# Lightning attention followed by a gated MLP on one core: a new instruction order, and DMA transposes for the last four steps

## The chip, the core and the metric

The kernel runs on one core of a Trainium2 chip. The core has five engines that run side by side and meet through semaphores: PE (TensorE, matrix products), DVE (VectorE), ACT (ScalarE), POOL (GpSimd) and SP (SyncE, which here issues DMAs only). The metric is the device time of one execution in microseconds (us), less is better.

## The reference, cut to what matters

Inputs are q, k, v of shape (4 batches, 8 heads, 768 tokens, 64), one decay per head, and four weights. First comes an attention with decay, block by block; then a gated MLP in which one weight mixes the tokens.

```python
for b in range(nb):                       # blocks of 64 tokens
    intra = einsum('bhic,bhjc->bhij', qb, kb) * Dmask
    intra = einsum('bhij,bhjd->bhid', intra, vb)
    inter = einsum('bhid,bhde->bhie', qb * lam_pow, kv_state)
    out[:, :, sl] = intra + inter
    kv_state = lam_block * kv_state + einsum('bhsd,bhse->bhde', kb * rev_pow, vb)
x = attn_out.transpose(0, 2, 1, 3).reshape(B, S, H * D)
h = maximum(x @ w_in, 0); u, v = h[..., :512], h[..., 512:]
v_n = (v - mean(v)) / sqrt(var(v) + 1e-6)
v_s = einsum('ts,bsd->btd', w_spatial, v_n) + b_spatial[None, :, None]
return (u * v_s) @ w_out
```

## The kernel before

The work is cut into 12 steps n of 256 tokens, three for each of the four batches. The decay is put into the operands: v is scaled by a power per token, q by the inverse power, so that the state only adds up.

The order is written out by hand. `ORDER` is a string of tokens; the last letter names the engine (T is PE, D is DVE, A is ACT, P is POOL, S is SP) and the kernel emits the tokens as they stand, so that every engine runs its own tokens strictly in this order. A token that waits holds everything behind it on its engine. Data dependences and the reuse of buffers become semaphore waits.

A step goes as follows. `LK`, `LQ`, `LV` (L184) each load 512 KB of fp32 over SP's queue into one of three buffers per input. `KC`, `QC` (`split`, L263) cast k and q to bf16 in two halves, one instruction each; `VD` (L274) scales v. `TK`, `TQ` (L284) transpose k and q by eight matrix products each with the identity, into PSUM; `EK` copies kT out, `EQ` (L297) copies qT out and multiplies by the power `lq`. kT and qT have two buffers each. `SC` (L313, two halves of 16 products) makes the scores, `MK` (L317) masks them, `KV` (L329) adds to the state, `SS` copies the state out, `AV` (L350 and L359, two parts) makes the attention output, and `EX` copies it out as x transposed. `PV` (L385, four products of 512 columns) makes the v half of the first weight's product, `PU` (L423, eight of 256) the u half; `EV`, `EU` apply the maximum, and `BN`, `RA`, `RD`, `VN` normalize v.

Once for each batch, after its three steps: `PW` (L445, six products of 384 columns, eight tokens for a batch) mixes the tokens, `GB` adds the bias, `GM` (L456) multiplies by u, `PO` (L462, four products of 512 columns, six tokens) applies the last weight, `EO` copies out and `ST` stores 256 KB over SP's queue.

The first weight comes in two halves, `WI.0` (v half) and `WI.1`, the mixing weight in two, `WS.0` and `WS.1`, the last weight as `WO`. They go over POOL's queue and are cast on the way. Before each stands `GT.x.n`: a copy of one element of the loaded k (x = 0), q (x = 1) or v of step n, which makes POOL wait until that load has landed. `WT` (L435) transposes the mixing weight on PE. At the very start stand the constants: `lam`, `pos`, `idn`, `msk`, and `LB` to `LT`, which make the tables of powers.

Of the kernel before, what the change touches and what calls it, by code (L numbers as in the profile page):

```python
# [21 lines left out]
TQ.2.3.T EK.2.6.A EQ.2.3.D AV.1.0.0.T KV.1.0.T SC.2.1.2.T SC.2.0.4.T SS.1.0.A MK.2.1.2.D KV.1.1.T AV.1.1.0.T  # L22
SS.1.1.A EX.1.1.1.A MK.2.0.4.D LK.5.2.S VD.2.2.P PV.0.1.6.T EX.1.0.0.D PV.0.0.1.T EV.0.1.6.A PV.1.1.0.T
BN.0.1.D PV.1.0.6.T EV.0.0.1.D EV.1.1.0.A BN.0.0.D AV.2.0.2.T EV.1.0.6.A PU.1.1.5.T BN.1.1.D RA.0.A BS.S
GT.0.3.P WS.1.P KV.2.0.T BN.1.0.D PU.1.0.6.T KC.3.2.A SS.2.0.D RD.0.D LK.4.2.S PU.0.0.4.T VN.0.1.D QC.3.2.P
EU.1.1.5.A VN.0.0.D AV.2.1.2.T RA.1.A EU.0.0.4.A GT.1.3.P WS.0.P TK.3.5.T RD.1.D VN.1.0.D EX.2.1.3.A TQ.3.1.T
# [20 lines left out]
EX.6.1.1.A ST.0.3.S TQ.8.6.T RD.5.D MK.7.0.2.D PU.6.1.1.T LK.10.2.S PV.6.0.0.T VN.5.1.D EU.6.1.1.A QC.10.2.P
VN.5.0.D PV.6.1.3.T LK.8.2.S EQ.8.6.D EV.6.0.0.A VD.7.2.P MK.7.1.4.D PW.1.0.1.1.T PU.6.0.6.T LV.11.2.S
BN.6.0.D QC.9.2.P LV.10.2.S PW.1.1.0.0.T GB.1.0.1.1.D EU.6.0.6.A EV.6.1.3.D GM.1.0.1.P PW.1.0.0.6.T
GB.1.1.0.0.D BN.6.1.D GM.1.1.0.P PW.1.2.1.5.T GB.1.0.0.6.D RA.6.A PW.1.3.0.4.T RD.6.D GM.1.0.0.P GB.1.2.1.5.D  # L50
# [459 lines left out]
```

## Time and profile before

| | |
|---|---|
| median of 3 runs | 160.79 us (159.54 to 161.46) |
| the profiled execution | 161.64 us, its span 159.9 us |
| mean granted TensorE clock | 0.979 |
| moved by DMA | 28.63 MB, mean 179 GB/s |
| HBM read, written | 24.77 MB, 6.29 MB |

The span runs from the first to the last instruction of the profiled execution; 1.74 us of that execution lie outside it. Busy time is the union of an engine's instructions. A "[idle before <- releaser]" behind an instruction says how long its engine was idle before it and what ended that.

### The profile page before, as it was taken

How to read it: one execution, taken by the hardware profiler on the slowest of the kernel's cores; microseconds unless marked ns; L12 is line 12 of the kernel's file. 1: busy time of each engine (PE TensorE's matmuls, PEld its weight loads, DVE VectorE, ACT ScalarE, POOL GpSimd, SP SyncE). 2: the span in 40 equal slices, each digit the busy share in tenths (PEclk: the TensorE clock that was granted, in tenths of full speed). 3: DMA queues.
4: the chain of work that ended last, by engine and by line, in shares of the span. 5: the costliest groups of instructions: out<-in, count | busy, mean ns of one | idle time of the engine just before them, and what ended most of it. 6: DMA issues, size and time to landing. Idle time of an engine off the chain costs nothing.

```text
span 159.9 us, 4876 instructions
## 1 busy us (share of the span) xinstructions
PE 138.3 (86%) x2073; PEld 91.0 (57%) x2090; DVE 108.2 (68%) x191; ACT 82.4 (52%) x154; POOL 77.7 (49%) x91
## 2 busy tenths in 40 slices
...
GB/s 104 298 290 290 291 226 230 231 315 237 298 243 240 288 269 235 56 236 195 277 331 318 287 165 71 196 135 0 4 0 6 4 0 4 64 148 186 0 197 197
DMA packets 43448, 28.63 MB, mean 179 GB/s; under 512 B 1058, under 2 KB 40226, under 8 KB 43426
## 3 DMA queue, kind: packets, MB, share of 16 engines
...
q0 software_dynamic: 2384, 2.75, 10.0%
...
q10 hardware_dynamic: 2, 0.00, 0.0%
HBM read 24.77 MB, written 6.29 MB: 194 GB/s over the span
## 4 chain that ended last, share of the span: by engine, by line
PE 54%; DMA 15%; DVE 12%; SPq 5%; POOL 5%; issue 4%; ACT 3%; DVEq 0%; ACTq 0%; POOLq 0%
PE ps L462 13%; PE ps L423 11%; PE ps L385 10%; PE ps L445 8%; DMA win_sb<-in_moe_w_in_dram 6%; SPq L184 5%; DMA q_in<-in_q_dram 5%; DMA k_in<-in_k_dram 5%; POOL gT L456 4%; DVE vsb L450 4%; PE ps L284 3%; DVE vn L414 3%; PE ps L313 2%; PE ps L329 2%; PE ps L359 2%
## 5 line engine op out<-in xcount | busy, mean ns | idle before, releaser
L456 POOL TENSOR_TENSOR gT<-vsb,uT 128x384 bf16<-128x384 f32 x28 | 30.1, 1096 | 28.5 <-DVE vsb L450 23.6
L445 PE MATMUL ps<-wt_sb,vn 128*128 128x384 bf16 x192 | 33.7, 326 | 0.2 <-DVE vsb L450 0.2
L317 DVE TENSOR_TENSOR a_sb<-ps,m 128x1024 bf16<-128x1024 f32 x24 | 28.7, 1218 | 6.0 <-PE ps L313 5.0
L276 POOL TENSOR_TENSOR vd<-v_in,lv 128x1024 bf16<-128x1024 f32 x12 | 22.8, 1904 | 16.0 <-DMA q_in<-in_q_dram 6.4
L385 PE MATMUL ps<-win_sb,xT 128*128 128x512 bf16 x85 | 24.9, 412 | 4.1 <-DMA win_sb<-in_moe_w_in_dram 3.3
L445 PEld LDWEIGHTS <-vn 128*128 128x128 bf16 x192 | 18.2, 98 | 11.9 <-issue 0.4
L423 PE MATMUL ps<-xT,win_sb 128*128 128x256 bf16 x192 | 24.2, 273 | 0.3 <-DVE wt_sb L170 0.3
L168 ACT ACTIVATE o_sb<-ps 128x512 f32<-128x512 f32 x21 | 12.6, 599 | 20.6 <-PE ps L462 17.3
L400 DVE BATCH_NORM_STATS2 st<-vh 128x6 f32<-128x512 bf16 x24 | 16.6, 690 | 9.7 <-ACT vh L390 9.5
L462 PE MATMUL ps<-wout_sb,gT 128*128 128x512 bf16 x90 | 21.6, 379 | 0.3
L450 DVE TENSOR_TENSOR vsb<-ps,bsp 128x384 f32<-128x384 f32 x32 | 17.3, 549 | 5.6 <-PE ps L445 5.1
L423 PEld LDWEIGHTS <-win_sb 128*128 128x128 bf16 x192 | 17.8, 98 | 3.6 <-issue 0.6
L390 ACT ACTIVATE vh<-ps 128x512 bf16<-128x512 f32 x18 | 10.8, 601 | 15.4 <-PE ps L385 15.4
L390 ACT ACTIVATE uT<-ps 128x512 bf16<-128x512 f32 x22 | 12.9, 600 | 10.1 <-PE ps L423 10.1
L385 PEld LDWEIGHTS <-xT 128*128 128x128 bf16 x96 | 9.5, 104 | 14.0 <-issue 6.6
L414 DVE TENSOR_SCALAR vn<-vh,mv,rstd 128x512 bf16<-128x512 bf16 x24 | 16.5, 723 | 0.3
L172 POOL CAST qc<-q_in 128x512 bf16<-128x512 f32 x16 | 9.4, 616 | 14.9 <-DMA q_in<-in_q_dram 10.5
L462 PEld LDWEIGHTS <-gT 128*128 128x128 bf16 x96 | 9.1, 98 | 10.2 <-POOL gT L456 0.3
L168 ACT ACTIVATE xT<-ps 128x512 bf16<-128x512 f32 x19 | 10.7, 597 | 6.4 <-PE ps L359 6.3
L172 POOL CAST kc<-k_in 128x512 bf16<-128x512 f32 x14 | 8.2, 614 | 11.7 <-DMA k_in<-in_k_dram 5.3
L297 DVE TENSOR_TENSOR qT<-ps,lq 128x1024 bf16<-128x1024 bf16 x12 | 8.2, 681 | 7.4 <-ACT kT L168 3.3
L284 PE MATMUL ps<-ident,kc 128*128 128x128 bf16 x96 | 8.2, 235 | 4.7 <-ACT kc L168 4.3
...
## 6 DMA issues: line engine op xcount, KB each, us to landing
k_in<-in_k_dram SPq DMA_DIRECT2D x12, 512.0 KB, 7.4
q_in<-in_q_dram SPq DMA_DIRECT2D x12, 512.0 KB, 7.8
v_in<-in_v_dram SPq DMA_DIRECT2D x12, 512.0 KB, 8.6
out_dram<-o_sb SPq DMA_DIRECT2D x24, 256.0 KB, 2.1
wsp_raw<-in_moe_w_spatial_dram POOLq DMA_DIRECT2D x2, 576.0 KB, 10.0
win_sb<-in_moe_w_in_dram POOLq DMA_DIRECT2D x2, 512.0 KB, 10.2
wout_sb<-in_moe_w_out_dram POOLq DMA_DIRECT2D x1, 512.0 KB, 8.8
bsp<-in_moe_b_spatial_dram SPq DMA_DIRECT2D x1, 384.0 KB, 10.0
```

The costliest lines, as they stand in the source:

```text
L168: nc.scalar.activation(out=o, in_=i, func=AF.Copy)
L172: nc.gpsimd.tensor_copy(out=o, in_=i)
L276: vec(e).tensor_tensor(out=vd[n % NCA][:, h], in0=v_in[n % NIN][:, h], in1=lv[:, n % NR, h].unsqueeze(3).broadcast_to((P, h.stop - h.start ...
L317: nc.vector.tensor_tensor(out=a_sb[n % NA][:, i].rearrange("p o w j x -> p (o w) (j x)"), in0=bank(b, 2).rearrange("p o (w y) -> p (o w) y ...
L385: nc.tensor.matmul(out=bank(b), lhsT=x[:, c, g], rhs=win_sb[:, g, DH:DFF], start=(g == 0), stop=(g == NCH - 1))
L390: nc.scalar.activation(out=o, in_=i, func=AF.Relu)
L414: vec(e).tensor_scalar(out=vn[p2][:, t], in0=vh[p2][:, t], scalar1=mv[p2][:, t, 0:1], scalar2=rstd[p2][:, t:t + 1], op0=ALU.subtract, op1= ...
L423: nc.tensor.matmul(out=pu[:, f2].rearrange("p (c x) -> p c x", c=2), lhsT=win_sb[:, g, f * P:(f + 1) * P], rhs=x[:, :, g, :], start=(g == ...
L445: nc.tensor.matmul(out=bank(b)[:, 0:HW], lhsT=vn[bb % 2][:, s, f * P:(f + 1) * P], rhs=wt_sb[:, s, i * HW:(i + 1) * HW], start=(s == 0), s ...
L450: nc.vector.tensor_tensor(out=vsb[(bb * 4 + f) % NVS][:, i * HW:(i + 1) * HW], in0=bank(b)[:, 0:HW], in1=bsp[:, i * HW:(i + 1) * HW], op=A ...
L456: vec(e).tensor_tensor(out=gT[bb % 2][:, f, cols].rearrange("p (a y m) -> p a y m", m=2, y=Q64), in0=vsb[(bb * 4 + f) % NVS][:, cols].rear ...
L462: nc.tensor.matmul(out=bank(b), lhsT=gT[bb % 2][:, f, t * P:(t + 1) * P], rhs=wout_sb[:, f, :], start=(f == 0), stop=(f == NCH - 1))
```

## The change

The whole `ORDER` is written anew. In it:

- The loads start with `LK.0 LQ.0 LK.1 LV.0 LK.2 LQ.1 LQ.2 LV.1 LV.2`, where before they started with `LK.0 LQ.0 LV.0 LV.1 LK.1 LQ.1 LK.2 LQ.2 LV.2`. `WI.0` and `WI.1` wait for `LQ.1`, `WS.1` and `WS.0` for `LQ.2`; before, `WI.0` waited for `LK.2`, `WI.1` for `LQ.2`, `WS.1` for `LK.3`, `WS.0` for `LQ.3`.
- `QC` of steps 0, 1, 2 and 7 and `KC` of step 9 are on DVE; before, no `KC` or `QC` was. `KC` and `QC` are one instruction over all heads where they were two.
- In steps 8 to 11 `TK`, `EK`, `TQ`, `EQ` are gone. `DK` and `DQ` transpose k and q from SBUF to SBUF by DMA, issued by SP, straight into kT and qT. `QM` (two tokens per step, POOL six times and DVE twice) casts q and multiplies it by a power per token, from a new table `lqn`, in the place of `QC` and of the product in `EQ`.
- The layout of `kc` and `qc` has two axes exchanged, so that a partition's row of them holds the blocks of 128 columns one behind the other.
- The mask is set on POOL and goes first there; its copies have a token of their own (`mkc`).
- The last tile of the output is copied out in two halves on ACT and DVE (`EH`) and stored in two halves from the queues of ACT and SP (`SH`).

The diff, with the orders cut to the start, the stretch with the DMA transposes, and the end:

```diff
-LK.0.2.S lam.A pos.P LQ.0.2.S LV.0.2.S LV.1.2.S idn.P LB.6.T msk.P LN.6.A LK.1.2.S KC.0.2.A LL.D LX.A TK.0.6.T
-LQ.1.2.S QC.0.2.P EK.0.6.D LT.0.A TQ.0.6.T LK.2.2.S VD.0.2.P LT.1.A EQ.0.6.D SC.0.1.0.T LT.2.A LQ.2.2.S
-SC.0.0.2.T VD.1.2.P MK.0.1.0.D MK.0.0.2.D LV.2.2.S KC.1.2.P AV.0.0.0.T KV.0.0.T LK.3.2.S TK.1.6.T QC.1.2.A
-SS.0.0.A TQ.1.5.T EK.1.6.A KV.0.1.T LQ.3.2.S GT.0.2.P WI.0.P EQ.1.5.D AV.0.1.0.T SS.0.1.A EX.0.1.1.A
-SC.1.0.2.T KC.2.2.P SC.1.1.4.T EX.0.0.0.A MK.1.0.2.D LV.3.2.S QC.2.2.A GT.1.2.P WI.1.P TK.2.6.T MK.1.1.4.D
...
+LK.0.2.S lam.A msk.P LQ.0.2.S LK.1.2.S idn.P mkc.D LV.0.2.S LB.6.T pos.P LN.6.A LK.2.2.S LL.D KC.0.2.P LX.A
+LQ.1.2.S TK.0.6.T LT.0.A QC.0.2.D LQ.2.2.S TQ.0.5.T EK.0.6.A EQ.0.5.D KC.1.2.A SC.0.0.0.T LV.1.2.S SC.0.1.2.T
+LT.2.A MK.0.0.0.D TK.1.6.T VD.0.2.P EK.1.6.A MK.0.1.2.D LV.2.2.S LT.1.A AV.0.0.0.T LK.3.2.S KV.0.0.T SS.0.0.A
+GT.1.1.P WI.0.P QC.1.2.D KV.0.1.T AV.0.1.0.T KC.2.2.A LQ.3.2.S GT.1.1.P WI.1.P TQ.1.6.T EX.0.1.1.A TK.2.5.T
+EQ.1.6.D GT.1.2.P WS.1.P EX.0.0.0.A QC.2.2.D EK.2.5.A SC.1.0.2.T LQ.4.2.S GT.1.2.P WS.0.P SC.1.1.0.T
+MK.1.0.2.D TQ.2.6.T SS.0.1.A VD.1.2.P EQ.2.6.D MK.1.1.0.D SC.2.0.2.T SC.2.1.4.T MK.2.0.2.D AV.1.0.0.T KV.1.0.T
+LV.3.2.S MK.2.1.4.D SS.1.0.A KV.1.1.T VD.2.2.P AV.1.1.0.T SS.1.1.A PV.0.0.6.T EX.1.1.1.A EX.1.0.0.A PV.0.1.1.T
+EV.0.0.6.A AV.2.0.2.T BN.0.0.D PV.1.1.6.T EV.0.1.1.D KV.2.0.T BN.0.1.D PV.1.0.5.T SS.2.0.A EV.1.1.6.D RA.0.A
...
+QC.7.2.D GM.1.0.1.P KV.6.1.T AV.6.1.0.T GB.1.1.0.6.D KC.8.2.A PW.1.2.0.5.T EX.6.0.0.D DQ.8.S GM.1.1.0.P
+EX.6.1.1.A SS.6.1.D PW.1.2.1.6.T DK.8.S GB.1.2.0.5.D VD.8.2.P PW.1.3.0.5.T GB.1.2.1.6.D LK.11.2.S PU.6.0.6.T
+GB.1.3.0.5.D GM.1.2.0.P TQ.7.4.T GM.1.3.0.D EU.6.0.6.A GM.1.2.1.P PU.6.1.5.T EQ.7.4.D LV.11.2.S QM.9.0.P
+PO.1.0.6.T EU.6.1.5.A SC.7.0.0.T VD.7.2.P EO.1.0.6.A SC.7.1.2.T PO.1.2.5.T MK.7.0.0.D LQ.10.2.S PV.6.1.6.T
+MK.7.1.2.D QM.9.1.P PO.1.1.4.T LV.10.2.S EV.6.1.6.A EO.1.2.5.D AV.7.0.0.T BN.6.1.D EO.1.1.4.A SC.8.1.2.T
+SC.8.0.5.T KV.7.0.T MK.8.1.2.D PV.6.0.4.T ST.1.1.S SS.7.0.A KV.7.1.T MK.8.0.5.D EV.6.0.4.A AV.7.1.0.T
+PW.1.1.1.3.T SS.7.1.A ST.1.0.S VD.9.2.P EX.7.1.1.D AV.8.0.4.T EX.7.0.0.D GB.1.1.1.3.D KV.8.0.T DQ.9.S
+PU.7.1.6.T KC.9.2.D SS.8.0.A GM.1.1.1.P KC.10.2.A BN.6.0.D AV.8.1.4.T QM.10.1.P PV.7.0.3.T EU.7.1.6.A DK.9.S
+QM.10.0.D EX.8.0.4.A DK.10.S PV.7.1.6.T RA.6.A VD.10.2.P EV.7.0.3.A RD.6.D VN.6.1.D DQ.10.S EX.8.1.5.A
+PW.1.3.1.2.T BN.7.0.D PV.8.1.3.T EV.7.1.6.D GB.1.3.1.2.D PV.8.0.6.T ST.1.2.S EV.8.1.3.A BN.7.1.D GM.1.3.1.P
+PU.7.0.2.T EV.8.0.6.A BN.8.1.D QM.11.0.P RA.7.A PO.1.3.3.T BN.8.0.D EU.7.0.2.A QM.11.1.P PO.1.5.6.T VN.6.0.D
+EO.1.3.3.A RD.7.D RA.8.A VN.7.1.D SC.9.0.0.T ST.1.3.S EO.1.5.6.A SC.9.1.2.T VN.7.0.D PO.1.4.5.T MK.9.1.2.D
+ST.1.5.S PU.8.1.6.T EO.1.4.5.A RD.8.D MK.9.0.0.D PU.8.0.4.T ST.1.4.S EU.8.1.6.A VN.8.0.D AV.9.0.0.T EU.8.0.4.A
+VN.8.1.D SC.10.1.2.T SC.10.0.5.T KV.9.0.T MK.10.1.2.D PW.2.0.0.4.T SS.9.0.A MK.10.0.5.D KV.9.1.T AV.9.1.0.T
+KC.11.2.A PW.2.1.0.3.T DQ.11.S VD.11.2.P GB.2.0.0.4.D SS.9.1.D EX.9.0.0.A DK.11.S PW.2.1.1.6.T GB.2.1.0.3.D
+EX.9.1.1.A PV.9.0.5.T GM.2.0.0.P GB.2.1.1.6.D PU.9.1.4.T GM.2.1.1.P EV.9.0.5.A PV.9.1.6.T BN.9.0.D GM.2.1.0.P
+EU.9.1.4.A PW.2.3.1.5.T EV.9.1.6.A BN.9.1.D PW.2.3.0.6.T GB.2.3.1.5.D RA.9.A AV.10.0.0.T GB.2.3.0.6.D
+GM.2.3.1.P SC.11.0.2.T SC.11.1.4.T RD.9.D KV.10.0.T MK.11.0.2.D PU.9.0.6.T SS.10.0.A VN.9.1.D KV.10.1.T
...
+EO.3.3.4.A PO.3.5.6.T ST.3.3.S EO.3.4.5.A ST.3.4.S EH.3.5.6.0.A EH.3.5.6.1.D SH.3.5.0.A SH.3.5.1.S
...
+    lqn = sb([P, NR, H, 2], FP32, "lqn")
...
-    kc = many(NCA, [P, 2, 4, 2, D], BF16, "kc")
-    qc = many(NCA, [P, 2, 4, 2, D], BF16, "qc")
+    kc = many(NCA, [P, 4, 2, 2, D], BF16, "kc")
+    qc = many(NCA, [P, 4, 2, 2, D], BF16, "qc")
...
     def l_x(e):
+        nc.scalar.activation(out=lqn, in_=lv, func=AF.Exp, scale=-1.0)
         nc.scalar.activation(out=lv, in_=lv, func=AF.Exp)
...
     def c_mask(e):
-        nc.vector.memset(mfull, 1.0)
+        nc.gpsimd.memset(mfull, 1.0)
         nc.gpsimd.affine_select(out=mfull, in_=mfull, compare_op=ALU.is_ge, fill=0.0, base=0,
                                 pattern=[[-1, 2], [1, 2], [2, P]], channel_multiplier=-2)
+
+    def c_mask2(e):
         for c in range(2):
             rows = slice(c * Q64, (c + 1) * Q64)
...
     def split(e, n, x, src, dst):
-        for o in ((0, 1) if x == 2 else (x,)):
-            copy(e, dst[n % NCA][:, :, :, o, :].rearrange("p m u d -> p u m d"),
-                 src[n % NIN][:, 4 * o:4 * o + 4])
+        copy(e, dst[n % NCA].rearrange("p u m o d -> p o (u m) d"),
+             src[n % NIN].rearrange("p (o u) m d -> p o (u m) d", o=2))
...
+    def q_m(e, n, o):
+        vec(e).tensor_tensor(out=qc[n % NCA][:, :, :, o].rearrange("p u m d -> p (u m) d"),
+                             in0=q_in[n % NIN][:, 4 * o:4 * o + 4].rearrange("p u m d -> p (u m) d"),
+                             in1=lqn[:, n % NR, 4 * o:4 * o + 4].rearrange("p u m -> p (u m)").unsqueeze(2)
+                             .broadcast_to((P, 8, D)), op=ALU.mult)
+
+    def d_k(e, n):
+        nc.sync.dma_start_transpose(kT[n % NTR].rearrange("p u m x -> p (u m) x"),
+                                    kc[n % NCA].rearrange("p u m o d -> p (u m o d)"))
+
+    def d_q(e, n):
+        nc.sync.dma_start_transpose(qT[n % NTR].rearrange("p u m x -> p (u m) x"),
+                                    qc[n % NCA].rearrange("p u m o d -> p (u m o d)"))
...
-                nc.tensor.transpose(out=pt[:, u, m], in_=src[n % NCA][:, m, u].rearrange("p o d -> p (o d)"),
+                nc.tensor.transpose(out=pt[:, u, m], in_=src[n % NCA][:, u, m].rearrange("p o d -> p (o d)"),
...
-                    nc.tensor.matmul(out=pkv[row(o), u], lhsT=kc[n % NCA][row(c), m, u, o, :],
+                    nc.tensor.matmul(out=pkv[row(o), u], lhsT=kc[n % NCA][row(c), u, m, o, :],
...
+    def e_h(e, bb, t, b, x):
+        half = slice(x * (DM // 2), (x + 1) * (DM // 2))
+        copy(e, o_sb[(bb * NT + t) % NO][:, half], bank(b)[:, half])
+
+    def s_h(e, bb, t, x):
+        half = slice(x * (DM // 2), (x + 1) * (DM // 2))
+        eng = {"S": nc.sync, "A": nc.scalar}[e]
+        eng.dma_start(out=out[bb, t * P:(t + 1) * P, half], in_=o_sb[(bb * NT + t) % NO][:, half])
...
```

## Rows read from the trace of the kernel before

**Rows 1.** The page, part 1: busy us (share of the span) xinstructions of each engine.

```profile
PE 138.3 (86%) x2073; PEld 91.0 (57%) x2090; DVE 108.2 (68%) x191; ACT 82.4 (52%) x154; POOL 77.7 (49%) x91
```

**Rows 2.** Windows: stretch, length, each engine's busy time (instructions), clock, DMA share, GB/s.

```profile
0.00:25.90 25.90, 11.57 (x299) 9.76 (x300) 12.03 (x19) 15.95 (x31) 15.07 (x26) 0.97 1.05 248
25.90:32.10 6.20, 5.98 (x23) 2.16 (x27) 2.71 (x6) 1.19 (x2) 0.97 (x2) 0.58 1.16 236
32.10:156.20 124.10, 120.74 (x1760) 79.07 (x1776) 93.42 (x167) 64.67 (x120) 61.69 (x64) 1.00 0.57 161
```

**Rows 3.** The timeline of PE, start to 32 us: start, length, instruction [idle before it].

```profile
6.59 1.04 PE L284 MATMUL ps<-ident,kc 128*128 128x128 bf16 x8 [3.92 <-ACT kc L168]
...
18.54 0.62 PE L284 MATMUL ps<-ident,kc 128*128 128x128 bf16 x8 [0.35 <-POOL kc L172]
...
22.18 0.43 PE L359 MATMUL ps<-a_sb,vd 64*64 64x128 bf16 x14
25.90 0.58 PE L385 MATMUL ps<-win_sb,xT 128*128 128x512 bf16 x1 [3.29 <-DMA win_sb<-in_moe_w_in_dram]
26.70 5.38 PE L385 MATMUL ps<-win_sb,xT 128*128 128x512 bf16 x14 [0.22 <-issue]
```

**Rows 4.** The timelines of ACT and of POOL, start to 36 us.

```profile
5.38 1.15 ACT L168 ACTIVATE kc<-k_in 128x512 bf16<-128x512 f32 x2 [2.50 <-DMA k_in<-in_k_dram]
...
14.42 1.15 ACT L168 ACTIVATE qc<-q_in 128x512 bf16<-128x512 f32 x2 [1.55 <-DMA q_in<-in_q_dram]
...
16.38 0.93 POOL L236 DMA_DIRECT2D win_sb<-in_moe_w_in_dram  x1
...
21.10 1.90 POOL L276 TENSOR_TENSOR vd<-v_in,lv 128x1024 bf16<-128x1024 f32 x1 [1.75 <-DMA v_in<-in_v_dram]
...
31.13 1.16 POOL L172 CAST qc<-q_in 128x512 bf16<-128x512 f32 x2 [7.09 <-DMA q_in<-in_q_dram]
```

**Rows 5.** DMA queues in 22 to 26 us: packets, MB, share of 16 engines.

```profile
q0 software_dynamic: 564, 0.56, 82.4%
q1 hardware_dynamic: 564, 0.29, 34.8%
```

**Rows 6.** DMA queue q0 in 20 to 21 us, the first in which it has any.

```profile
q0 software_dynamic: 106, 0.11, 64.7%
```

**Rows 7.** The chain of waits, in order of time, far stretches: start, length, what.

```profile
102.73 0.86 PE ps L385 x4
103.59 0.45 PE ps L284 x8
...
120.26 0.22 PE ps L313 x16
...
127.34 0.98 PE ps L423 x8
128.32 0.97 PE ps L445 x6
...
133.55 1.73 PE ps L462 x8
...
156.26 0.60 ACT o_sb L168
```

**Rows 8.** DMA issues: size, median us from issue to landing.

```profile
v_in<-in_v_dram SPq DMA_DIRECT2D x12, 512.0 KB, 8.6
out_dram<-o_sb SPq DMA_DIRECT2D x24, 256.0 KB, 2.1
```

**Rows 9.** Groups by line: out<-in, shapes, count | busy, mean ns of one | idle before.

```profile
L317 DVE TENSOR_TENSOR a_sb<-ps,m 128x1024 bf16<-128x1024 f32 x24 | 28.7, 1218 | 6.0 <-PE ps L313 5.0 <-ACT uT L390 0.9
L276 POOL TENSOR_TENSOR vd<-v_in,lv 128x1024 bf16<-128x1024 f32 x12 | 22.8, 1904 | 16.0 <-DMA q_in<-in_q_dram 6.4 <-PE ps L329 5.3 <-DMA v_in<-in_v_dram 4.0
...
L297 DVE TENSOR_TENSOR qT<-ps,lq 128x1024 bf16<-128x1024 bf16 x12 | 8.2, 681 | 7.4 <-ACT kT L168 3.3 <-PE ps L284 2.5 <-ACT lq L215 1.4
...
L170 DVE CAST xT<-ps 128x512 bf16<-128x512 f32 x5 | 3.3, 683 | 2.1 <-PE ps L359 2.1
```

More of the change, by code (lines that the diff above doesn't have):

```diff
@@ L22 @@
[L22 to L26, printed above, removed]
@@ L47 @@
[L47 to L50, printed above, removed]
-VN.6.0.D KC.8.2.A PW.1.1.1.6.T GM.1.2.1.P VN.6.1.D GB.1.3.0.4.D LK.11.2.S TK.8.5.T GB.1.1.1.6.D GM.1.3.0.P
@@ new lines @@
+EX.2.0.2.A PU.1.1.5.T EU.0.1.4.A EU.1.0.6.D PV.2.0.3.T RA.1.A VN.0.1.D EU.1.1.5.A RD.1.D TK.3.6.T VN.1.1.D
+EV.2.0.3.A PU.2.0.2.T VN.1.0.D EK.3.6.A BN.2.0.D PV.2.1.3.T EU.2.0.2.A PU.2.1.6.T EV.2.1.3.A LK.4.2.S WT.3.2.T
+BN.2.1.D EU.2.1.6.A QC.3.2.P WT.4.3.T WT.0.5.T EW.3.2.D RA.2.A WT.1.6.T LK.5.2.S EW.4.3.D EW.0.5.A WT.5.4.T
+WT.2.2.T RD.2.D VN.2.1.D EW.5.4.A TQ.3.3.T QC.4.2.P VN.2.0.D PU.0.0.5.T EW.2.2.A EQ.3.3.D LQ.6.2.S EW.1.6.A
+TQ.4.4.T VD.3.2.P SC.3.1.0.T EU.0.0.5.A EQ.4.4.D SC.3.0.2.T PW.0.0.1.6.T LQ.5.2.S MK.3.1.0.D PW.0.1.1.5.T
@@ new lines @@
+GB.0.0.1.6.D LV.4.2.S MK.3.0.2.D PW.0.1.0.4.T GM.0.0.1.P KC.4.2.A PW.0.0.0.6.T GB.0.1.1.5.D GB.0.1.0.4.D
+LK.6.2.S GM.0.1.1.P TK.4.5.T GB.0.0.0.6.D PW.0.2.1.4.T GM.0.1.0.P EK.4.5.D LK.7.2.S AV.3.0.0.T GT.0.5.P WO.P
+GB.0.2.1.4.D SC.4.0.2.T SC.4.1.5.T KV.3.0.T MK.4.0.2.D PW.0.3.1.4.T GM.0.2.1.P SS.3.0.A LV.6.2.S QC.6.2.P
+MK.4.1.5.D KV.3.1.T AV.3.1.0.T KC.5.2.A PW.0.3.0.3.T GM.0.0.0.P SS.3.1.D GB.0.3.1.4.D LV.5.2.S QC.5.2.A
+TK.5.6.T EX.3.1.1.D GM.0.3.1.P PW.0.2.0.2.T GB.0.3.0.3.D EX.3.0.0.A VD.4.2.P EK.5.6.A GM.0.3.0.D TQ.5.3.T
@@ new lines @@
+GB.0.2.0.2.D PV.3.1.5.T EQ.5.3.D PU.3.0.6.T EV.3.1.5.A GM.0.2.0.P AV.4.0.0.T BN.3.1.D EU.3.0.6.A SC.5.1.2.T
+SC.5.0.4.T LQ.8.2.S KV.4.0.T MK.5.1.2.D PV.3.0.6.T SS.4.0.A MK.5.0.4.D KV.4.1.T EV.3.0.6.A AV.4.1.0.T LK.8.2.S
+KC.6.2.P PO.0.0.3.T EX.4.0.0.A BN.3.0.D EX.4.1.1.A PO.0.1.6.T EO.0.0.3.D RA.3.A LK.9.2.S PV.4.0.2.T RD.3.D
+SS.4.1.D EO.0.1.6.A VN.3.1.D VD.6.2.P VN.3.0.D PV.4.1.3.T EV.4.0.2.A ST.0.0.S TK.6.6.T BN.4.0.D EV.4.1.3.A
+PO.0.2.2.T EK.6.6.A BN.4.1.D VD.5.2.P TQ.6.3.T LV.9.2.S EO.0.2.2.A PU.3.1.5.T EQ.6.3.D RA.4.A PO.0.3.6.T
```

70 lines of the change are left out of this document (21 added, 49 removed).

## The prediction

> **What bounds the kernel now.** I read the page first: PE is busy for 138.3 us of 159.9, far more than any other engine [rows 1]. That share is an average, so the windows come next. Up to 25.9 us PE works for 11.57 us while the DMA share is above 1: the loads set the pace. From 25.9 to 32.1 us PE is busy, but at a granted clock of 0.58. From 32.1 to 156.2 us it is busy for 120.74 of 124.10 us at full clock, while the DMA share falls to 0.57: here PE's own work sets the pace, and all its idle time is 3.36 us [rows 2]. So there are three places to win or lose: the start, the amount of work on PE, and the tail.
>
> PE's timeline shows what ends the start. The attention of steps 0 and 1 is done at 22.6; then PE waits 3.29 us for the v half of the first weight. After that gap the clock is low, and 14 products of `PV` take 5.38 us [rows 3]; at full clock four take 0.86 [rows 7], so 14 take 3.0.
>
> That weight was issued at 16.38 and used at 25.90, 9.5 us later [rows 3, 4]. The queues say why: between 22 and 26 us both have moved 564 packets [rows 5]. They take turns packet by packet, and a weight's packet lands 1 KB of bf16 where a load's lands 512 bytes. A load of 1024 packets takes 1.8 us on the quiet queue (k of step 0 has landed at 5.38, the sixth load, q of step 1, at 14.42 [rows 4]: 9.04 / 5 = 1.8), but 1024 / 141 = 7.3 us beside a weight.
>
> **The start, walked with these landings.** The loads keep their steps of 1.8 us: k0 5.4, q0 7.2, k1 9.0, v0 10.8, k2 12.6, q1 14.4, q2 16.2, v1 18. `WI.0` now waits for the sixth load instead of the seventh and is issued at 14.5 instead of 16.38; with the same 9.5 us it can be used at 24.0. `WI.1` and both `WS` follow within 4 us. The weights' first packets came 3.9 us after their issue (in the 21st us [rows 4, 6]), so now they stand beside the loads from about 18.3 us on: 7.3 us for the 1024 packets of the two `WI`, and for the two `WS` 768 packets, half as long again, at an estimated 141 / 1.5 = 94 per us, 8.2 us. v of step 2, which had landed at 21.10 [rows 4], now lands at about 25.5, k of step 3 at about 34.
>
> On PE the same work precedes the first `PV` in both orders: the attention of steps 0 and 1, the scores of step 2. DVE paces it, which now also has `QC` of steps 0 to 2. No row has a DVE cast of this shape out of SBUF; half of it out of PSUM takes 0.683 [rows 9], so the bounds are 1.37 and, at twice that rate, 0.68; I take 1.1, nearer to the row. When q1 lands at 14.4, DVE has two `QC`, two `EQ` and four masks before it: 2.2 + 1.4 + 4.9 [rows 9] = 8.5 us, with an estimated 1.5 us of waits for ACT and PE 24.4; the second mask of step 1 is ready at 22, and `AV.1.1` ends at 23.9. So weight and attention are ready together, PE has no gap of 3 us before `PV`, and I let the clock stay up. The next token but one is `AV.2.0`. It needs `VD.2`, 1.90 us on POOL [rows 9] behind v's landing, and so 27.5 to 28; PE arrives at 25.8. A new wait of 2 us stands there, with all of PE behind it. `TK.3` may be late by 1 us (k3 at 34, its cast 1.2, PE there at 34.4); that I leave to the range.
>
> The gain, counted to the state "16 products of `PV` done": 32.1 before, 24.0 + 16 x 0.215 + 2 = 29.4 now, so 2.7 us.
>
> **PE's work.** Steps 8 to 11 lose eight groups of eight transposes. A group lengthens the chain by 0.45 us [rows 7]; PE is busy there, so 8 x 0.45 = 3.6 us are gained, if what takes their place is in time. `EK` and `EQ` of these steps leave ACT and DVE, and `QM` costs on POOL about half of `VD`, 0.95 each [rows 9]. Neither engine is the bound there (DVE 93 of 124 us, POOL 62 [rows 2]), so I cost this at nothing; without that cover the two `QM` and `KC.9` on DVE would cost 2 to 3 us. The other reordering after 32 us also goes at nothing: at most the 3.36 us of idle time can be won, and as much can come back.
>
> **The DMA transposes.** The trace has none. Of transfers near in size it shows a store of 256 KB, landed 2.1 us after its issue, and a load of 512 KB, twice the bytes and beside others, 8.6 us [rows 8]. Their result is only awaited, so they can gain nothing beyond the 3.6 us. I take 3 us each, near the store: same bytes, same queue, and little other traffic this late.
>
> Their cover I count in PE's groups (`PW` 0.97, `PU` 0.98, `PV` and `PO` 0.86, a half of `SC` 0.22, `AV` taken as 0.45 [rows 7]). Step 8: `DQ.8` must wait until `AV.6.1` has read the buffer; then come three `PW`, `TQ.7`, two `PU`, three `PO`, `PV.6.1`, both halves of `SC.7` and `AV.7.0` before `SC.8`: 9.7 us for two transposes. Steps 9 and 10: from `KC.9`, which waits for `GB.1.1.1`, to `SC.10` there are 11.3 us for three (`DK.9`, `DK.10`, `DQ.10`; `DQ.9` goes ahead). Step 11: from `AV.9.1` to `SC.11` four `PW`, two `PV`, a `PU` and `AV.10.0`, 7.0 us for two. So they are hidden if each adds at most 4.9, 3.8 and 3.5 us. Queued behind them on SP are the loads of k, v of step 11 and q, v of step 10, and the stores; `VD.10` and `QM.10` come about 8 us after the issue of their loads, as long as a median landing [rows 8].
>
> **The tail.** After 156.26 `EO` takes 0.60, then a store of 2.1 us lands [rows 7, 8]. Halves on two engines and two queues save about 0.2 us of the copy.
>
> **The sum**, against the profiled execution: 161.64 - 2.7 (start) - 3.6 (transposes) - 0.2 (tail) = 155.1. That execution lies 0.85 us above the median of the three runs, inside their spread of 1.9 us; I predict 155.0.
>
> **Rivals.** First, the start gives nothing. The two `WS` moved forward starve v2, k3 and q3; before, q of step 3 landed only at 31.13 [rows 4] behind three weight halves. If the wait at `AV.2.0` is 4 us instead of 2 and `TK.3` adds 1, the start loses 3.0 us; if the clock is low there as well, another 2.4 (5.38 against 3.0). For it speaks that eight transposes took 1.04 us at 6.59 and 0.62 at 18.54, as at a low clock in the sparse beginning [rows 3], and that the new order works PE sparsely until 22 us. Against it: the gap of 3.29 us is gone. The time is then 158 to 160.5; I put it at 159.
>
> Second, and slower: the DMA transposes are late, and PE stands at `SC.8`, `SC.10` and `SC.11`. At 5 us each the waits are 0.3 + 3.7 + 3.0 = 7 us and the gain is just lost (162); at 6 us 2.3 + 6.7 + 5.0 = 14, hence 169; at the load's 8.6 us 7.5 + 14.5 + 10.2 = 32, hence 187. It decides from about 5.2 us each. Against it speaks the store's row; for it, that no row shows how fast SP hands out such a transfer.
>
> A page speaks for a far worse case of the same rival. The Trainium skill ("VectorE: DVE Perf Modes", section "The three transpose paths") gives 1309 ns for one 128x128 bf16 block through the DMA crossbar against 390 ns on TensorE, and its rules send this transpose to TensorE if PSUM will do. Eight blocks one behind the other would be, as an estimate from that page, 10.5 us per transpose, and by the same covers (11.3 + 20.2 + 14.0) the time would be about 201. No run here shows it; the sum stays as it is.
>
> Third, the new order is bound elsewhere, in DVE's chain or POOL's: PE's late idle time doubles from 3.4 to 7 us, and the time is 158.5.
>
> **How the numbers follow.** Forecast 0.57, around 155.1 with some 4 us to either side for the waits of the new order; the start gives nothing 0.19; transposes late 0.16, a quarter of that on the page's figure; bound elsewhere 0.08. The range leaves out most of the late transposes: low 150.5 (no wait at `AV.2.0` and most of the 3.36 us idle won), high 161.5. About 1% is what a measurement of this kernel can tell from no change, so the same is 159.2 to 162.4. Faster: 0.57 + 0.08 + half of the 0.19 = 0.75; same: the other half and a little of the late case, 0.11; slower 0.14.
>
> **What would show it.** In the profile after: `PV`'s first product at about 24 us and a clock of 1.0 from 24 to 32; a wait for `VD.2` before `AV.2.0` of about 2 us; no idle time of PE before the score products of steps 8 to 11; DMA transposes that land about 3 us after their issue; PE's work after that point 3.6 us shorter. I am wrong if PE waits at its score products for the DMA late in the run, or if it is idle for more than some 4 us between 24 and 45 us.

## The result, and the profile after

Four runs of the changed kernel have a median of 152.88 us (151.99 to 153.04), four of the kernel before beside them 160.16 (159.25 to 161.46). The ratio is 0.953, 95% interval 0.944 to 0.961: faster by 7.3 us in the medians. 155.0 was predicted. The profiled execution after took 152.98 us, its span is 151.2, against 161.64 and 159.9. The profiled execution before is slower than each of the 47 others that were timed of that kernel (158.69 to 161.59), so the 8.7 us between the two spans, which are split up below, are 1.4 more than the medians differ by.

The page's busy times and the same three stretches as in [rows 1, 2], cut where the changed kernel has its first `PV`, the state "16 products of `PV` done", and PE's last product (columns as there):

```profile
PE 133.6 (88%) x2026; PEld 87.2 (58%) x2026; DVE 106.9 (71%) x190; ACT 81.4 (54%) x146; POOL 75.6 (50%) x74
...
0.00:23.98 23.98, 12.65 (x298) 10.65 (x299) 12.70 (x19) 16.14 (x30) 14.72 (x24) 1.00 1.08 246
23.98:28.50 4.52, 4.52 (x56) 1.99 (x55) 2.72 (x6) 1.61 (x4) 0.01 (x1) 1.00 1.18 218
28.50:147.52 119.02, 116.45 (x1673) 74.57 (x1672) 91.06 (x165) 63.22 (x113) 60.82 (x50) 1.00 0.77 194
```

The second stretch, which ran at a clock of 0.58 before, runs at 1.00. The third has become 5.1 us shorter. First the start, on PE's timeline, then on POOL's:

```profile
22.77 0.43 PE L375 MATMUL ps<-a_sb,vd 64*64 64x128 bf16 x14
23.98 1.89 PE L401 MATMUL ps<-win_sb,xT 128*128 128x512 bf16 x8 [0.78 <-DMA win_sb<-in_moe_w_in_dram]
25.80 0.31 PE L366 MATMUL ps<-qT,s_sb 64*64 64x128 bf16 x8
25.93 0.39 PE L375 MATMUL ps<-a_sb,vd 64*64 64x128 bf16 x16
26.26 1.04 PE L401 MATMUL ps<-win_sb,xT 128*128 128x512 bf16 x4
27.23 0.44 PE L345 MATMUL ps<-vd,kc 64*64 64x64 bf16 x16
27.60 1.04 PE L401 MATMUL ps<-win_sb,xT 128*128 128x512 bf16 x4
28.57 0.31 PE L366 MATMUL ps<-qT,s_sb 64*64 64x128 bf16 x8
```

```profile
14.65 0.93 POOL L239 DMA_DIRECT2D win_sb<-in_moe_w_in_dram  x1
...
20.86 1.90 POOL L292 TENSOR_TENSOR vd<-v_in,lv 128x1024 bf16<-128x1024 f32 x1 [0.64 <-DMA v_in<-in_v_dram]
```

`PV` starts at 23.98 and the eight products before `AV.2.0` take 1.89 us, where 14 took 5.38 [rows 3] (15 of the 16 before have a record). `AV.2.0` at 25.80 waits for nothing: `VD.2` ran from 20.86 to 22.76.

The DMA transposes, from the list of DMA issues (median us to landing in the last column), and the score products of steps 8 to 11 on PE's timeline:

```profile
qT<-qc SPq DMA_TRANSPOSE x4, 3.2
kT<-kc SPq DMA_TRANSPOSE x4, 3.6
```

```profile
89.52 0.62 PE L329 MATMUL ps<-qT,kT 64*64 64x128 bf16 x32
...
102.34 0.64 PE L329 MATMUL ps<-qT,kT 64*64 64x128 bf16 x32
...
105.88 0.65 PE L329 MATMUL ps<-qT,kT 64*64 64x128 bf16 x32
...
115.45 0.62 PE L329 MATMUL ps<-qT,kT 64*64 64x128 bf16 x32
```

None of them has a bracket, so PE waited for none. The last transpose before each landed 3.2, 3.6, 4.0 and 2.2 us ahead of it (`DK.8` issued at 82.56 landed 3.8 later, `DK.9` 94.73 + 4.0, `DQ.10` 98.67 + 3.2, `DK.11` 110.18 + 3.1).

What idle time PE has left after 30 us, on its timeline:

```profile
54.41 0.64 PE L329 MATMUL ps<-qT,kT 64*64 64x128 bf16 x32 [0.69 <-DVE qT L313]
65.08 0.42 PE L375 MATMUL ps<-a_sb,vd 64*64 64x128 bf16 x16 [0.59 <-POOL vd L292]
68.85 0.61 PE L300 MATMUL ps<-ident,kc 128*128 128x128 bf16 x8 [1.23 <-DVE a_sb L333]
```

And the tail:

```profile
147.60 0.38 ACT L168 ACTIVATE o_sb<-ps 128x256 f32<-128x256 f32 x1 [0.27 <-PE ps L478]
148.01 0.42 DVE L170 COPY o_sb<-ps 128x256 f32<-128x256 f32 x1 [5.09 <-ACT o_sb L168]
```

The two halves are not copied side by side: DVE starts when ACT has ended.

The span's 8.7 us come together so. The state "16 products of `PV` done" is reached at 28.5 instead of 32.08, with 0.8 us of work (`AV.2.0` from 25.80 to 26.26, `KV.2.0` from 27.23 to 27.60) already done that came after it before: 4.4. PE's work from there on: 120.76 against 116.45 + 0.8: 3.5. Its idle time there: 3.36 against 2.57: 0.8. From PE's last product to the end of the span: 3.7 in both. Sum 8.7.

The split is that of one pair of executions. A second profiled execution of the changed kernel (beside the last of the experiments) has a span of 151.5. Its `PV` starts at 24.45, its first eight products take 3.1 us although the granted clock reads 1.00, and the state is reached at 30.3, 1.8 us later; counted in the same way the start gives 2.6. The span is only 0.3 longer: the waits of 0.59 and 1.23 us above are not there, and one of 0.82 is new. Another run with the same start (the first of the two on the tail, below) has the granted clock at 0.50 from 24 to 26, with no gap ahead of `PV`. A line from either, the second execution first:

```profile
25.28 2.37 PE L401 MATMUL ps<-win_sb,xT 128*128 128x512 bf16 x6 [0.22 <-issue]
```

```profile
23.84 3.19 PE L402 MATMUL ps<-win_sb,xT 128*128 128x512 bf16 x8
```

The eight products that took 1.89 us above take 3.19 in that run. So the full rate at `PV` is not certain with this start, and the gap before it is not all that decides it.

### The profile page after: what moved, and what is told of

It reads as the page before. It is cut to its first block, busy times and chain, and to the rows that moved or that the text cites. A ratio compares the mean times of both kernels' runs of the same rounds, so it can differ in the third digit from the quotient of the medians.

```text
span 151.2 us, 4756 instructions
## 1 busy us (share of the span) xinstructions
PE 133.6 (88%) x2026; PEld 87.2 (58%) x2026; DVE 106.9 (71%) x190; ACT 81.4 (54%) x146; POOL 75.6 (50%) x74
## 4 chain that ended last, share of the span: by engine, by line
PE 70%; DMA 16%; DVE 5%; SPq 4%; issue 2%; POOL 0%; ACT 0%; ACTq 0%
PE ps L461 20%; PE ps L439 13%; PE ps L401 13%; PE ps L478 11%; DMA q_in<-in_q_dram 10%; DMA win_sb<-in_moe_w_in_dram 6%; SPq L184 4%; PE ps L375 3%; PE ps L345 3%; PE ps L329 3%; PE ps L300 2%; PE ps L366 2%; PE ps L451 1%; DVE vsb L466 1%; DVE vn L430 1%
## 5 line engine op out<-in xcount | busy, mean ns | idle before, releaser
L401 PE MATMUL ps<-win_sb,xT 128*128 128x512 bf16 x96 | 23.6, 380 | 0.8 <-DMA win_sb<-in_moe_w_in_dram 0.8
L478 PE MATMUL ps<-wout_sb,gT 128*128 128x512 bf16 x96 | 23.4, 380 | 0.0
L439 PEld LDWEIGHTS <-win_sb 128*128 128x128 bf16 x192 | 18.3, 98 | 4.4
L168 ACT ACTIVATE o_sb<-ps 128x512 f32<-128x512 f32 (+1 forms) x21 | 12.3, 586 | 14.9 <-PE ps L478 10.7
L406 ACT ACTIVATE vh<-ps 128x512 bf16<-128x512 f32 x21 | 12.5, 597 | 13.6 <-PE ps L401 13.6
L401 PEld LDWEIGHTS <-xT 128*128 128x128 bf16 x96 | 8.8, 98 | 9.6 <-issue 0.8
L168 ACT ACTIVATE s_sb<-ps 128x256 bf16<-128x256 f32 x14 | 5.3, 381 | 16.1 <-PE ps L345 16.1
L430 DVE TENSOR_SCALAR vn<-vh,mv,rstd 128x512 bf16<-128x512 bf16 x24 | 12.5, 551 | 0.3
L375 PE MATMUL ps<-a_sb,vd 64*64 64x128 bf16 x384 | 11.1, 225 | 1.7 <-DVE a_sb L333 1.0
L168 ACT ACTIVATE kc<-k_in 128x1024 bf16<-128x1024 f32 x7 | 7.4, 1056 | 8.4 <-PE ps L345 5.1
L329 PE MATMUL ps<-qT,kT 64*64 64x128 bf16 x384 | 8.4, 233 | 2.5 <-DVE qT L313 2.5
```

The lines of the kernel that those rows point to most:

```text
L168: nc.scalar.activation(out=o, in_=i, func=AF.Copy)
L375: nc.tensor.matmul(out=po[row(w), c ^ o, c, i], lhsT=vd[n % NCA][row(c), 4 * o + u, j, :], rhs=a[row(c), i, o, w, j, :], start=(r == 0 and ...
L401: nc.tensor.matmul(out=bank(b), lhsT=x[:, c, g], rhs=win_sb[:, g, DH:DFF], start=(g == 0), stop=(g == NCH - 1))
L406: nc.scalar.activation(out=o, in_=i, func=AF.Relu)
L439: nc.tensor.matmul(out=pu[:, f2].rearrange("p (c x) -> p c x", c=2), lhsT=win_sb[:, g, f * P:(f + 1) * P], rhs=x[:, :, g, :], start=(g == ...
L478: nc.tensor.matmul(out=bank(b), lhsT=gT[bb % 2][:, f, t * P:(t + 1) * P], rhs=wout_sb[:, f, :], start=(f == 0), stop=(f == NCH - 1))
```

## The experiments

Times are medians, ratios are to the kernel before on the same chip; lines are from one profiled execution of each run. "The changed kernel" has 152.9 us and a ratio of 0.953.

**The transposes back on PE, in the new order.**

```diff
-... QM.8.0.D QM.8.1.P ... DQ.8.S ... DK.8.S
+... QC.8.2.P ... TQ.8.3.T EQ.8.3.D ... TK.8.2.T EK.8.2.A        (steps 9 to 11 alike)
```

> The changed kernel, but k and q of steps 8 to 11 are transposed on TensorE again (QC on POOL, TK and TQ where the DMA transposes were issued, EK on ACT, EQ on DVE). Theory (TensorE's work is what ends last there): eight groups of 0.45 us come back, so 3.6 us more than the changed kernel's 152.9, 156.5 us, with TensorE's idle time after 30 us unchanged at about 2.6 us. Rival (the new order alone made the late stretch faster and the transposes fall into idle time): 152.9 to 153.9. Rival (what counts is the relief of DVE and ACT from EK and EQ, 1.02 and 0.68 us each): more than 3.6, 158 or above, with new idle time of TensorE in front of the score products.

Measured: 159.37 us, ratio 0.992 (0.987 to 0.997), 6.5 more than the changed kernel. The profiled execution, with 158.25 the fastest of ten, has a span of 156.5, 5.3 longer than with the DMA transposes. PE's last product ends at 152.88 instead of 147.52. Over the two parts of its run that compare (start of the stretch to 80, 80 to near the end) the windows of the changed kernel and then of this one say:

```profile
28.50:80.00 51.50, 48.94 (x805) 33.80 (x805) 41.01 (x73) 31.62 (x55) 25.31 (x22) 1.00 1.06 272
80.00:147.50 67.50, 67.50 (x870) 40.77 (x868) 50.06 (x93) 31.60 (x59) 35.50 (x29) 1.00 0.55 135
```

```profile
28.50:80.00 51.50, 50.47 (x818) 35.19 (x824) 41.99 (x75) 32.61 (x56) 27.23 (x24) 1.00 1.12 286
80.00:152.00 72.00, 68.18 (x903) 42.54 (x911) 49.47 (x93) 33.95 (x60) 30.92 (x25) 1.00 0.26 84
```

With the DMA transposes PE has no idle time at all after 80 us; without them 3.8, the longest of it 0.94 us for ACT's copy of xT, 0.63 for DVE's vh and 1.25 for DVE's vsb. Before 80 it is the other way round, 2.6 against 1.0. From 28.5 on that makes 3.1 us more work and 2.3 us more idle time. The releasers are ACT's and DVE's copies, the engines that `EK` and `EQ` burden again; which token pushed which was not separated. The time is that of the third expectation, but its waits in front of the score products are not there. The prediction had the work and had put the relief at nothing. The run shows one thing more: the new order with its new start, without the DMA transposes, is only 0.8% faster than the order before. `PV` starts as early there (24.02, granted clock 1.00), but from 28.5 to PE's last product it takes 124.4 us, as long as the kernel before took from 32.08.

**How much time the DMA transposes have.** Each is issued twice, the first time into a spare tile.

```diff
+        nc.sync.dma_start_transpose(spareT..., kc[n % NCA]...)     # in d_k, ahead of the real one
+        nc.sync.dma_start_transpose(spareT..., qc[n % NCA]...)     # in d_q
```

> The changed kernel, with each of the eight DMA transposes issued a second time, first into a spare tile that nobody reads. Theory (each adds 1.3 to 1.9 us to SP's queue, as its issue does in the changed kernel's trace, and the last one of a step lands 3.3 us after its issue): the pair of step 8 is ready at about 91.4 where SC.8 stands at 89.5, step 10 at about 108.4 against 105.9, step 11 at about 117 against 115.5, each wait pushing the rest: 4 to 6 us more than 152.9, 157 to 159. Rival (the cover is much longer than counted, or transposes run side by side): 153 to 154.

Measured: 163.26 us, ratio 1.013 (1.007 to 1.019). PE's timeline at `SC.8`, `SC.9` and `SC.10`:

```profile
89.93 0.64 PE L334 MATMUL ps<-qT,kT 64*64 64x128 bf16 x32 [1.55 <-DMA kT<-kc]
...
105.74 0.64 PE L334 MATMUL ps<-qT,kT 64*64 64x128 bf16 x32 [2.89 <-DMA kT<-kc]
...
113.59 0.64 PE L334 MATMUL ps<-qT,kT 64*64 64x128 bf16 x32 [4.15 <-DMA qT<-qc]
```

8.6 us of waits, where 4 to 6 were expected, and after the last of them the clock was 0.79 from 114 to 122. The last transpose before `SC.8` landed at 89.9 instead of 86.4, 3.5 us later with two more ahead of it. What one transpose adds can't be read from this: all eight spare ones write the same tile, and SP stood 5.1 us in all until the spare before had landed there, a wait that the changed kernel does not have. What the run shows is that the covers suffice for the eight transposes and not for sixteen, and that PE then does stand at its score products. So the slower rival is real, and its condition was not met.

**DMA transposes in the old order.** Each stands where its transposes on PE or its copies stood.

```diff
-TQ.8 ... EQ.8 ... TK.8 ... EK.8 ... QC.8       (of the order before, steps 8 to 11)
+              DQ.8 ...          DK.8 ... QM.8.0.P QM.8.1.P
```

> The kernel before with the DMA transposes of steps 8 to 11 alone: its order stays, DK and DQ stand where EK and EQ stood, QM on POOL where QC was, TK and TQ are gone. Theory (a DMA transpose needs cover: 3 to 4 us from issue to landing against some 1.2 for TK and EK): 3.6 us of TensorE's work are won, and TensorE waits 2 to 4 us at SC.8 and at SC.9 and about 1 at SC.11, so 159 to 161, no gain on 160.2. Rival (only TensorE's work counts, waits are filled): 156.6. Rival (the transposes, waiting in order on SP, hold up the loads of steps 10 and 11 behind them): 163 or more.

Measured: 173.13 us (170.41 to 174.04), span 171.2, 12 more than the theory's highest. In this run `DQ.8` stands behind `QM.10`, which writes the same buffer: step 8 is computed with the q of step 10, and `DQ.8` waits for the load of that. So it was run once more with `DQ.8` at the old place of `TQ.8`:

> DMA transposes in the old order again, each where its transposes on PE or its copies stood, but now DQ.8 at the place of TQ.8, so that it doesn't wait for the QM.10 that overwrites its source. Nothing of the computation is changed. Theory, that the transposes need the steps that the new order puts between them and their score products: waits of 3 to 5 us for kT or qT at SC.8 and at SC.9 or SC.10, 164 to 170 us. Rival, that the 173 us came from the misplaced DQ.8 alone: 156 to 159 us.

Measured: 173.39 us, ratio 1.084 (1.076 to 1.092). The misplaced token was not the reason, and the theory's 170 is passed too: PE stands at the score products for 3.84 and 1.06 us, but once for 7.07 us elsewhere, and the granted clock is 0.88 and 0.86 in the two stretches of 20 us from 80 on. The lines on POOL, DVE and PE around the longest gap:

```profile
88.75 2.04 POOL L274 TENSOR_TENSOR qc<-q_in,lqn 128x512 bf16<-128x512 f32 x2 [5.63 <-DMA qT<-qc]
90.75 1.90 POOL L289 TENSOR_TENSOR vd<-v_in,lv 128x1024 bf16<-128x1024 f32 x1
92.61 2.04 POOL L274 TENSOR_TENSOR qc<-q_in,lqn 128x512 bf16<-128x512 f32 x2
94.61 6.39 POOL L469 TENSOR_TENSOR gT<-vsb,uT 128x384 bf16<-128x384 f32 x6
```

```profile
95.73 0.56 DVE L463 TENSOR_TENSOR vsb<-ps,bsp 128x384 f32<-128x384 f32 x1 [6.20 <-POOL gT L469]
```

```profile
98.49 1.76 PE L458 MATMUL ps<-wt_sb,vn 128*128 128x384 bf16 x5 [7.07 <-DVE vsb L463]
```

Read from below: PE waits for `GB` on DVE, DVE for `GM` on POOL, and POOL had stood 5.63 us at `QM.10`, which may not write `qc` before `DQ.8` has read it. Behind it `VD`, `QM.9` and six `GM` were queued. The wait for the landing is paid by the engine that reuses the source, not at the score product only. In the new order `QM.10` stands some 15 us behind `DQ.8`. So what the transposes win is won by them and by the new order together; in the old order they cost some 13 us. How much of that the loads behind them on SP cost was not separated.

**The start alone, in the old order.** The first nine loads, the gates of `WI.0` and `WI.1` and the place of `VD.1` as in the new order, all else as before.

```diff
-LK.0 LQ.0 LV.0 LV.1 LK.1 LQ.1 LK.2 LQ.2 LV.2 ... GT.0.2.P WI.0.P ... GT.1.2.P WI.1.P
+LK.0 LQ.0 LK.1 LV.0 LK.2 LQ.1 LQ.2 LV.1 LV.2 ... GT.1.1.P WI.0.P ... GT.1.1.P WI.1.P VD.1.2.P
```

> The kernel before with the start alone: the first nine loads in the new order, both halves of the first weight released by q of step 1, VD.1 behind them on POOL; all else as before. Theory: PV starts at about 24 instead of 25.9 and the clock stays up, so 14 products take 3.0 instead of 5.4 us: 1.9 + 2.4 = 4.3 us less than 160.2, 155.9. Rival (the clock falls nevertheless): 158.3. Rival (given back later, as the loads of step 3 and the mixing weight come no earlier): 160.

Measured: 161.18 us, ratio 1.005 (1.000 to 1.010). `PV` starts at 24.06 and its 16 products run at full clock, as in the changed kernel's first profile; but the gain is given back, as the last expectation had it, most of it here:

```profile
42.67 2.99 PE L432 MATMUL ps<-ident,wsp_raw 128*64 128x128 bf16 x72 [2.35 <-DMA wsp_raw<-in_moe_w_spatial_dram]
```

PE comes 4 us earlier to the transposes of the mixing weight, whose second half was issued only at 31.20, behind the load of q of step 3. The clock is 0.79 from 40 to 48, and the `PU` that began at 48.85 before begins at 48.15. To see whether that is the whole of it, the same with `WS.1` and `WS.0` right behind `WI.1`, as in the new order:

> The old order with the new start as in the run of the start alone, and with the two halves of the spatial weight issued right behind WI.1, as the new order does, not behind the loads of step 3. Theory, that the start's gain was given back at the transposes of the spatial weight, which waited 2.35 us for their load: no wait for wsp_raw is left, the clock stays up, and 4 us of the start remain, less 1 us at SC.3, since q of step 3 now lands beside the weight: 157 us. Rival, that the old order gives the gain back anywhere: 160 to 161 us, with new waits for k or q of step 3.

Measured: 161.41 us, ratio 1.011 (1.006 to 1.015); the theory falls, the rival holds. The wait for `wsp_raw` is gone, and two others stand there:

```profile
22.73 0.42 PE L356 MATMUL ps<-a_sb,vd 64*64 64x128 bf16 x16 [2.18 <-POOL vd L273]
...
36.79 0.62 PE L281 MATMUL ps<-ident,qc 128*128 128x128 bf16 x8 [2.27 <-POOL qc L169]
```

The first is `AV.1.0`, and it is of my making: I had put both `WS` ahead of `VD.1` on POOL, as the new order has them, and in the old order `KC.2` there had already waited 1.79 us. The second is `TQ.3`, whose q landed only at 35.56, beside the weights. After the first the clock is low again (0.72 from 24 to 30). The new order has the same late q (35.64), but there `TQ.3` comes after `PU`, `PV` and `WT`. In these two runs loads and weights moved alone gain nothing; that PE's tokens are what was lacking is my reading, for no run moves them alone.

**The first weight later, in the new order.** One load later (behind q of step 2), and two (behind v of step 1).

```diff
-GT.1.1.P WI.0.P ... GT.1.1.P WI.1.P
+GT.1.2.P WI.0.P ... GT.1.2.P WI.1.P        (second run: GT.2.1.P twice)
```

> The changed kernel, with both halves of the first weight released by q of step 2 (7th load) instead of q of step 1 (6th). Theory: they are issued 1.7 us later, PV starts at about 25.6 instead of 24.0, and the time is 1.6 us longer, 154.5, if the clock stays up in a gap of 2.4 us; if the clock falls in it as it did in the kernel before in its gap of 3.3 us, 14 products cost 2.4 us more, 157. Rival (the start is hidden, later waits take it up): 153.

> The changed kernel, with both halves of the first weight released by v of step 1 (8th load). Theory: PV starts at about 27.4, a gap of 4.2 us in which the granted clock falls as in the kernel before: 3.4 us for the wait and 2.4 for the low clock, 158.7. Rival (the clock does not matter there, only the wait): 156.3. Rival (hidden): 153.

Measured: 154.56 us, ratio 0.962 (0.954 to 0.969), with `PV` at 25.43; 155.38 us, ratio 0.968 (0.961 to 0.974), with `PV` at 26.48. With one load the granted clock stays at 1.00, though the first eight products take 2.7 us (1.8 in the changed kernel's first profile), and `PV` 1.5 us later cost 1.7 in the median; the intervals of the two ratios overlap, and the profiled execution, with 152.90 the fastest of the four, is as fast as the changed kernel's. With two the time is 0.9 below even the lower of the expectations with a wait, 156.3, although the clock falls, as in the windows of 24 to 28 us:

```profile
24.00:26.00 2.00, 1.52 (x72) 1.34 (x60) 0.00 (x0) 0.77 (x2) 1.91 (x2) 0.68 1.20 218
26.00:28.00 2.00, 1.48 (x7) 0.66 (x5) 0.00 (x0) 1.08 (x2) 0.70 (x1) 0.50 1.19 215
```

but the wait ahead of it is not only that for the weight: `AV.1.0` waited 2.23 us for `VD.1`, which stands behind the later weights on POOL. From 20 to 24 us PE was busy for 1.18 us, and from 26 to 30 the granted clock is 0.50, the lower of its two levels (1.2 GHz). The state "16 products of `PV` done" is reached at 33.4, 4.9 us later than in the changed kernel's first profile, but the span is 2.6 longer: of the waits of 2.5 us that PE had there after 30 us, 0.7 is left. So a later start is in part taken up by later waits, and what the low clock costs in the end this run does not show. By the medians one load later costs 1.7 us and two 2.5, not the whole of the start.

**v of step 2 behind k of step 3.** This makes the wait that the prediction had feared.

```diff
-LV.2.2.S LK.3.2.S
+LK.3.2.S LV.2.2.S
```

> The changed kernel, with the loads of v of step 2 and k of step 3 exchanged. Theory: v of step 2 then has all its 1024 packets beside the weights' and lands at about 28.5 instead of 20.9; VD.2 ends at about 30.5, TensorE stands before AV.2.0 from 25.8 to 30.5, and as it works strictly in order the time is about 4.7 us longer, 157.6. Rival (TensorE's later idle time of 2.6 us takes up a part): 155 to 156. Rival (as my prediction had it, v of step 2 is late in the changed kernel already, and the exchange costs only the difference of 3 us): 156.

Measured: 157.09 us, ratio 0.978 (0.972 to 0.985).

```profile
30.56 0.64 PE L373 MATMUL ps<-a_sb,vd 64*64 64x128 bf16 x16 [4.31 <-POOL vd L290]
```

v lands at 28.60, as k of step 3 did at 28.48 in the changed kernel, and PE waits 4.31 us; the granted clock is 0.50 from 30 to 34. The theory's 157.6 is nearly met. So the first rival's mechanism was a true one, a wait of 4 us and a low clock behind it, though at 157 and not at its 158 to 160.5: the place of one load decides it. It did not come about because v of step 2 was fetched in time.

**The tail, and three waits.** First the last half in a tile of its own, since both halves are written to one tile:

```diff
-        copy(e, o_sb[...][:, half], bank(b)[:, half])
+        copy(e, o_half if x else o_sb[...][:, half], bank(b)[:, half])
```

> The changed kernel, with the second half of the last output tile in an SBUF tile of its own. In the changed kernel's trace DVE's half copy starts at 148.01, when ACT's (147.60 to 147.98) is over. Theory (the two writes into one tile are ordered): now both run at once, the last store is issued 0.4 us earlier, the span is 150.8 instead of 151.2. Rival (the two reads of one PSUM bank exclude one another): still one behind the other, span 151.2.

Measured: 153.58 us (150.71 to 155.0), no ratio. DVE's half still begins when ACT's has ended, 5.09 us idle "<-ACT o_sb", so the tile was not the cause. Then also the last product in two halves in two banks of PSUM, and the causes of the later waits moved:

```diff
-PO.3.5.6.T ... EH.3.5.6.0.A EH.3.5.6.1.D
+PH.3.5.6.0.T PH.3.5.3.1.T ... EH.3.5.6.0.A EH.3.5.3.1.D
 QM.8.0.D behind MK.6.1.4.D, QM.8.1.P behind KC.7.2.P, LQ.11.2.S behind LV.7.2.S, VD.5.2.P ahead of VD.6.2.P
```

> The new order, with the causes of its two later waits moved out of the way and the tail divided. QM.8 on DVE, which waited for q of step 8, goes behind MK.6.1, and the load of q of step 11 goes behind v of step 7; VD.5 goes ahead of VD.6; the last product of PO is made as two halves in two banks of PSUM, the second copied into a tile of its own. If the waits are what the timeline says they are: 1.23 us at TK.7 and 0.59 us at the product behind VD.5 are gone, and the two half copies lie 0.4 us nearer to PE's last product: 152.9 - 2.2 = 150.7 us. Rival, the waits only move to the next late tile (as waits have so far after each edit): 152 to 153 us, with PE idle as long elsewhere.

> The changed kernel once more, to stand beside the others on one chip: 152.9 us, ratio 0.953 to the kernel before.

Measured on one chip: 153.0 us, ratio 0.953 (0.945 to 0.960), against 151.85, ratio 0.951 (0.945 to 0.958) for the changed kernel. Nothing is won. DVE's half now begins on PE's release:

```profile
148.35 0.43 DVE L169 COPY o_half<-ps 128x256 f32<-128x256 f32 x1 [4.63 <-PE ps L483]
```

so it was the common bank that put the copies one behind the other. The releaser is a semaphore of ACT in the program; what the chip would do without it no run shows. DVE's half ends 0.46 us after PE's last product instead of 0.92, but the last stores took 2.1 us to land instead of 1.7. And the waits that I had moved were those of one execution. In the profile of the changed kernel's second execution these are all that PE has of 0.2 us or more after 30 us:

```profile
42.34 0.64 PE L329 MATMUL ps<-qT,kT 64*64 64x128 bf16 x32 [0.82 <-DVE qT L313]
57.01 0.64 PE L329 MATMUL ps<-qT,kT 64*64 64x128 bf16 x32 [0.63 <-DVE qT L313]
```

The 1.23 and 0.59 us are not there, with nothing changed.

## Why the prediction was right

The direction, the three places and the causes of the two large terms were right; the time came out 2.1 us below the forecast. By its steps:

- **The start** was put at 2.7 us and gave 4.4 in the first profile. `PV` at 24.0 was right. The term that failed is the wait of 2 us at `AV.2.0`: it measured 0, in the second execution too. I let v of step 2 land at 25.5, with all its 1024 packets beside the weight. It landed at 20.86. The queues show why, in 16 to 18, 18 to 19 and 20 to 21 us (q1 has the loads, q0 the weights):

```profile
q1 hardware_dynamic: 1123, 0.57, 116.7%
...
q1 hardware_dynamic: 302, 0.15, 63.3%
q0 software_dynamic: 100, 0.10, 61.0%
...
q0 software_dynamic: 142, 0.15, 85.3%
q1 hardware_dynamic: 140, 0.07, 34.6%
```

  Up to 18 us the loads' queue moved some 560 packets per us alone; then the two took turns at about 140 each, from 18.3 on if the weight's first 100 came at that rate. From 18 to 20.86 the loads' queue moved 302, 147 and some 120 packets. So, if the loads are served in order, about 450 of v's 1024 had passed before 18. The rate was right and so was the start of the race; only the position of v in the queue at that moment was not counted. k of step 3 landed at 28.48 for the same reason, not at 34. `QC` on DVE took 0.69 us, the lower bound, where I had taken 1.1. The clock that stays up was in part luck: it did so in both profiles of the changed kernel, but not in the first run on the tail, and the second profile lost 1.8 us there all the same.
- **How the gain is kept** I did not see, and here too I was lucky. The prediction walked the start up to the first `PU` and let the rest follow. The start alone, in the old order, gains the same there and has 0.7 us of it left 20 us later; the new order without the DMA transposes keeps 1.4 us of all. So 4.4 and 3.5 are shares of one sum, not what each part wins alone. My reading is that the new order has tokens in store for PE while the later loads come in; it was not tested by itself.
- **PE's work**: 3.6 predicted, 3.5 in the sum. Put back one for one in the new order, the transposes cost 5.3 of the span, 6.5 by the medians; the 2.3 us of idle time among the 5.3 stand behind copies of ACT and DVE, whose relief I had at nothing.
- **The DMA transposes**: 3 us each was taken; they landed 3.1 to 4.0 us after their issue, SP being held 1.2 to 2.8 by each, and all were hidden. The page of the Trainium skill that I set beside it ("VectorE: DVE Perf Modes", section "The three transpose paths") has 1309 ns for one block. Taken eight times, as I did, that does not agree with the trace: eight blocks in 3.1 to 4.0 us are at most 0.5 us for each.
- **Reordering** at nothing: the late idle time fell by 0.8 in this pair. **The tail** at 0.2: it measured 0. The two copies end 0.92 us after PE's last product, since they share a bank and so one followed the other, where one copy ended 0.67 after it; the smaller stores land that much sooner.

Against 155.1 - 1.74 = 153.4 for the span, the 2.2 us between forecast and measurement are 1.7 of the start, -0.1 of PE's work, 0.8 of idle time and -0.2 of the tail.
